# A third staging tile for the weight slices, scratch rows of the maxima moved into another tile, and a larger constant per transfer in the planner

## The chip, the cores and the metric

The kernel runs on one core of a Trainium2 chip. The metric is the device time of one execution in microseconds. The engines that matter are TensorE (PE, matmuls), VectorE (DVE), ScalarE (ACT), and SyncE (SP), whose queue issues every transfer of this kernel in program order.

## What is computed

An attention layer with a decay bias feeds two feed-forward layers with 2304 tokens, model width 512 and hidden width 2048. Cut to what matters:

```python
scores = scale * np.matmul(q, k.transpose(0, 1, 3, 2))          # 4 x 8 heads, 576 x 576, head width 64
bias = -(cum[:, :, :, None] - cum[:, :, None, :])               # cum: running sum of max(s, 0)
scores = np.where(causal, -1000000000.0, scores + np.minimum(bias, 0.0))
scores = scores - np.max(scores, axis=-1, keepdims=True)
attn = np.exp(scores)
attn = attn / (np.sum(attn, axis=-1, keepdims=True) + 1e-09)
x = np.matmul(attn, v)                                          # heads side by side: 2304 x 512
h = x @ w_in;  x = (h * np.cos(h)) @ w_out                      # first feed-forward layer
h = x @ w_in2; x = (np.maximum(h, 0.0) + np.log1p(np.exp(-np.abs(h)))) @ w_out2
```

## The kernel before, in words

The program is a list of operations (`P.op`), each with a due time `vt`, the tiles that it reads and writes, and one or two engines that may do it. `Planner.plan` turns this list into one instruction order for each engine: it steps through time with a cost for every operation and gives a free engine the ready operation with the earliest due time. On the chip only these orders remain: each engine works through its own in sequence and waits on semaphores where an input is late. For a transfer, the planner adds the time to issue it, 640 ns, its bytes at 360 per ns, and a constant (line 183, 770 ns) before it counts as landed.

Attention runs as 32 units (batch by head). For each unit PE makes the scores twice: once coarsely for the row maxima (line 510 on DVE: a masked maximum, with a scratch output in the tile `junk` that nobody reads; line 516 collects them), and once exactly for the exponential (line 564 on ACT). The product with v is copied out by line 538 (ACT, into `num`) and sent to the DRAM tile `adram`. After every fourth unit the sums of the rows come back as the tile `rd`, get 1e-9 added and are inverted (lines 591 and 592, DVE), and go out again. `emit_x` (lines 620, 298, 307) loads the normalised x for the feed-forward layers and splits it into a high and a low part, `xh` and `xl`.

A feed-forward layer works on token blocks of 512 (one of 256) and on 16 chunks `f` of the hidden width. For each chunk: 12 matmuls (w_in with xh and xl) into one of the banks that the program calls bank_65 to bank_68; an activation over several steps on ACT and DVE (layer one: lines 657, 658, 660, 662, 664; layer two: lines 669 to 676); its result is split into `ghi` (line 298, ACT) and `glo` (line 307, DVE); then 12 matmuls with w_out into bank_69 to bank_72. In the first layer the matmuls of a later chunk need the bank that line 664 has read.

The weights come in 64-bit slots of 1024 words of 32 bit (`wide`), 64 slices of 512 KB: 2 layers, 16 chunks, w_in and w_out. `emit_weights` turns each slice into a high and a low part: transfer into `stage`, then line 422 (ACT, absolute value, into `conv`), lines 424, 426, 429 and 432 (DVE), the high part (line 298, ACT) and the low part (line 307 or 308, DVE), into `wearly` or `wlate`. Slices take `stage` 0 and 1 in turn, so the transfer of a slice waits until line 432 has read the slice before the previous one. `conv` has two tiles too. The first layer's slices are worked through during attention and up to some 300 us; the second layer's replace the first's from 528 us on, chunk by chunk as the first layer's last block has used them.

Of the kernel before, what the change touches and what calls it, by code (L numbers as in the profile page):

```python
# [10 lines left out]
BF16 = mybir.dt.bfloat16  # L11
U32 = mybir.dt.uint32
# [10 lines left out]
QS = (0, 256, 576)  # L23
EARLY, SLOT = 8, 4992
GUARD = True
TUNE = dict(lam=61.3799, mu=21.9699, sub1=-0.8, sp4=-0.47, ld4=-2.57, load=-3.32, vload=0.3081, split=-0.462, max=-0.4135, s=1.63, av=2.34,
            norm=3.5, md=0.14, sd=0.22, ud=5900.0, e=1.2214, o=2.5648, end=3.5, x0=30.0, xd=2364.0, wa=5.755, wb=4.1769,
            wc=1479.6, wd=9828.5, wg=9000.0, pre=9606.0, we=16928.0, wf=6383.3, backlog=1292.7, hz=16175.7)
# [15 lines left out]
class Planner:  # L44
# [49 lines left out]
    def plan(self, penalty=4000.0):  # L94
# [7 lines left out]
        dma_free = 0.0  # L102
# [14 lines left out]
        while left:  # L117
            progress = False
            wake = []
            for e in free:  # L120
                if free[e] > t:
                    continue
                q = pend[e]
                while q and q[0][0] <= t:
                    _, sq, i, o = heapq.heappop(q)
                    if o.eng is None:
                        avail[e].append((o.vt, sq, i, o))
                a = [x for x in avail[e] if x[3].eng is None]
                avail[e] = a
                if not a:  # L130
                    if e == PE and self.filler and t >= self.filler_from:
                        o = Op()
                        o.seq, o.vt, o.eng, o.start, o.reads, o.writes, o.deps, o.succ = -1, t, PE, t, (), (("warm", 0),), set(), []
                        cold = t < self.filler_from + 5000.0
                        o.fn = self.filler
                        o.end = free[PE] = t + (215.0 if cold else 110.0)
                        tail = 107.0
                        order.append(o)
                        progress = True
                    continue  # L140
                if e in (DVE, ACT) and not force:
                    a = [x for x in a if x[0] <= reach + TUNE["hz"]]
                    if not a:
                        continue
                if e == PE and any(k == ("bank", 7) for k, _ in a[0][3].writes):
                    self.filler = None
                if e == SP and dma_free - t > TUNE["backlog"] + 0.01:
                    a = [x for x in a if x[3].opts[0][2].transfer < 300.0]
                    if not a:
                        wake.append(dma_free - TUNE["backlog"])  # L150
                        continue
                if e == ACT:
                    best = min(a, key=lambda x: (x[0] + (penalty if x[3].table and x[3].table != table else 0.0), x[1]))
                elif e == PE:
                    left_over = max(0.0, tail - (t - free[PE]))
                    fast = [x for x in a if x[3].opts[0][2].load < 100.0]

                    def score(x):
                        f = x[3].opts[0][2]
                        then = 54.0 if len(fast) > (f.load < 100.0) else LDW  # L160
                        return x[0] + TUNE["lam"] * max(0.0, f.load - left_over) + TUNE["mu"] * max(0.0, then - f.tail)

                    best = min(a, key=lambda x: (score(x), x[1]))
                else:
                    best = min(a, key=lambda x: (x[0], x[1]))
                _, _, i, o = best
                _, d, fn = o.opts[i]
                cost = d
                if e == PE:
                    reach = max(reach, o.vt)  # L170
                    cost += max(0.0, fn.load - left_over)
                    tail = fn.tail
                if e == ACT and o.table and o.table != table:
                    cost += self.SWITCH
                    table = o.table
                    switches += 1
                o.eng, o.fn, o.start = e, fn, t + (cost - d if e == PE else 0.0)
                free[e] = t + cost
                busy[e] += cost
                o.end = t + cost  # L180
                if e == SP:
                    dma_free = max(dma_free, t + d + 640.0) + fn.transfer
                    o.end = dma_free + 770.0
                order.append(o)
                left -= 1
                progress = True
                for s in o.succ:
                    s.ready = max(s.ready, o.end + min(self.hop(e, x[0]) for x in s.opts))
                    s.ndep -= 1
                    if s.ndep == 0:  # L190
                        push(s)
            if progress:
                force = False
            else:
                nxt = [f for f in free.values() if f > t]
                nxt += [pend[e][0][0] for e in free if pend[e] and pend[e][0][0] > t and free[e] <= t]
                nxt += wake
                force = not nxt
                if force:
                    continue  # L200
                assert nxt, [(o.vt, o.reads, o.writes) for o in ops if o.eng is None][:5]
                t = min(nxt)
# [22 lines left out]
def build(tc, qk, v, s, w1, w2, out):  # L225
# [8 lines left out]
    def T(name, shape, dt=F32):  # L234
        return sb.tile(shape, dt, name=name, tag=name)
# [8 lines left out]
    wide = w1.dtype != F32  # L244
# [5 lines left out]
    raws = [T(f"raw{i}", [128, 2, S]) for i in range(2)]  # L250
    xst = [raws[0][:, i, 0:512] for i in range(2)]
    rst = [raws[1][:, i, 0:512] for i in range(2)]
    stage = [T(f"stage{i}", [128, 1024], U32) for i in range(2)] if wide else []
    conv = [T(f"conv{i}", [128, 512], U32 if wide else F32) for i in range(2)]
    ghi = [T(f"ghi{i}", [128, 512], F32R) for i in range(2)]
    glo = [T(f"glo{i}", [128, 512], F32R) for i in range(2)]
# [4 lines left out]
    bc = T("bc", [128, 2, S])  # L261
# [6 lines left out]
    ident = T("ident", [128, 128], BF16)  # L268
    tri = T("tri", [128, 128], BF16)
    zero = T("zero", [128, 256], BF16)  # L270
    junk = [T(f"junk{i}", [128, (384, 512)[i]], BF16) for i in range(2)]
    mxp = T("mx", [128, 2, 10])
    mx = [mxp[:, i] for i in range(2)]
    mr = [xl[1][:, i, 0:128] for i in range(3)]
# [67 lines left out]
    for i in range(3):  # L342
        o = i * SLOT
# [31 lines left out]
    def warm():  # L375
# [14 lines left out]
         r=[(nk[0], "spos")], w=[(nk[1], "cum")])  # L390
# [6 lines left out]
    stage_n = [0]  # L397
# [9 lines left out]
    def emit_weights(which, f, at):  # L407
        w = (w1, w2)[which]
        tag = (which, f)
        for half, (hi, lo, scale, nm) in enumerate(((wih[f], wil[f], 2.0 if which else None, "wi"), (woh[f], wol[f], None, "wo"))):  # L410
            i = stage_n[0] % 2
            stage_n[0] += 1
            cv = conv[i]
            vs_ = at(f + half * 0.5)
            wsrc = w[f, :, half * 512:half * 512 + 512]
            if wide:
                sg = stage[i]
                dma(at(f + half * 0.5 - 0.7), sg, wsrc.bitcast(U32), r=[("go", 0)], w=[(("st", i), (tag, half))])
                pr = sg.rearrange("p (n t) -> p n t", t=2)
                cf = cv.bitcast(F32)  # L420
                if GUARD:
                    P.op(vs_ - 2, [(ACT, act_t(512), lambda cf=cf, pr=pr: A.activation(cf, pr[:, :, 1].bitcast(F32), AF.Abs))],  # L422
                         r=[(("st", i), (tag, half))], w=[(("cv", i), (tag, half, -2))])
                    P.op(vs_ - 1, [(DVE, dve_t(512, fast=True), lambda cf=cf: V.tensor_scalar(cf, cf, HI_MIN, HI_MAX, op0=ALU.max, op1=ALU.min))],
                         r=[(("cv", i), (tag, half, -2))], w=[(("cv", i), (tag, half, -1))])
                P.op(vs_, [(DVE, dve_t(512, fast=True), lambda cv=cv, hs=cv if GUARD else pr[:, :, 1]: V.tensor_scalar(  # L426
                    cv, hs, 3, 0x3FFFFFFF, op0=ALU.logical_shift_left, op1=ALU.bitwise_and))],
                    r=[(("st", i), (tag, half))] + ([(("cv", i), (tag, half, -1))] if GUARD else []), w=[(("cv", i), (tag, half, 0))])
                P.op(vs_ + 1, [(DVE, dve_t(512), lambda cv=cv, pr=pr: V.scalar_tensor_tensor(  # L429
                    cv, pr[:, :, 1], 0xC0000000, cv, op0=ALU.bitwise_and, op1=ALU.bitwise_or))],  # L430
                    r=[(("st", i), (tag, half)), (("cv", i), (tag, half, 0))], w=[(("cv", i), (tag, half, 1))])
                P.op(vs_ + 2, [(DVE, dve_t(512), lambda cv=cv, pr=pr: V.scalar_tensor_tensor(  # L432
                    cv, pr[:, :, 0], 29, cv, op0=ALU.logical_shift_right, op1=ALU.bitwise_or))],
                    r=[(("st", i), (tag, half)), (("cv", i), (tag, half, 1))], w=[(("cv", i), (tag, half))])
                src = cv.bitcast(F32)
            else:
                dma(at(f + half * 0.5 - 0.7), cv, wsrc, r=[("go", 0)], w=[(("cv", i), (tag, half))])
                src = cv
            sk = slot_keys(f) if which == 0 else []
            P.op(vs_ + 3, copy_opts(hi, src, 512, scale=scale, engines=(ACT,)),  # L440
                 r=[(("cv", i), (tag, half))], w=[((nm, "h", f), tag)] + sk)
# [353 lines left out]
```

## Time and profile before

| | |
|---|---|
| Runs | 1022.13, 1023.58, 1024.79 us; median 1023.58 |
| Profiled execution | 1024.17 us, of which 1022.4 us are the span from the first to the last instruction |
| PE | busy 1006.6 us (98% of the span) |
| DVE, ACT | busy 701.5 and 613.8 us (69% and 60%) |
| HBM | 66.87 MB read, 18.64 MB written |
| Mean granted clock of TensorE | 0.995 of 2.4 GHz |

An engine's busy time is the union of its instructions. A number in brackets behind an instruction is the time that its engine idled before it, with what ended the wait. PE's share hides that the span consists of stages with different limits, so the stages are what to read.

### The profile page before, as it was taken

What the parts mean: (1) busy time and instruction counts of PE and PEld (TensorE: products, weight loads), DVE (VectorE), ACT (ScalarE), POOL (GpSimd) and SP (SyncE); (2) the same over time, 40 slices, a digit from 0 to 9 for tenths busy, and PEclk for the clock granted to TensorE, in tenths of its full rate; (3) what the DMA queues carried; (4) which work ended last, traced back from release to release, by engine and by line L of the source; (5) the groups of instructions that cost most, each with busy time, mean ns of one, the idle gap of its engine ahead of it and who ended that gap; (6) DMA issues with size and microseconds to landing.
All of it is one profiled execution on the core that took longest, in us unless ns stands there. A gap on an engine that the chain in (4) does not pass through costs nothing.

```text
span 1022.4 us, 14520 instructions
## 1 busy us (share of the span) xinstructions
PE 1006.6 (98%) x5179; PEld 844.5 (83%) x5179; DVE 701.5 (69%) x1441; ACT 613.8 (60%) x1129; POOL 49.4 (5%) x67
## 2 busy tenths in 40 slices
PE   8999999999999999999999998999999999999998
PEld 7888788877888889988888886888888998888886
DVE  8799898969974545545458999975564756545553
ACT  4777777767765545555456668664455555554444
POOL 8112111100000000000000000000000000000000
PEclk9999999999999999999999999999999999999999
DMA  5766666773522222102014435310230200001001
GB/s 164 223 184 201 169 181 189 190 198 114 170 83 83 62 83 82 44 21 62 1 43 136 152 124 175 124 62 1 83 105 9 84 1 23 19 1 42 1 1 41
DMA packets 45098, 95.31 MB, mean 93 GB/s; under 512 B 7586, under 2 KB 14242, under 8 KB 45026
## 3 DMA queue, kind: packets, MB, share of 16 engines
q1 hardware_dynamic: 45026, 94.39, 30.4%
q8 instruction: 40, 0.66, 0.3%
q14 instruction: 32, 0.26, 0.1%
HBM read 66.87 MB, written 18.64 MB: 84 GB/s over the span
## 4 chain that ended last, share of the span: by engine, by line
PE 81%; DMA 8%; DVE 5%; ACT 3%; issue 2%; POOL 1%; SPq 0%; ACTq 0%; DVEq 0%; POOLq 0%
PE bank L321 80%; DMA stage<-w 5%; DMA adram<-num 2%; PE bank L376 1%; DMA rd<-adram 1%; DVE conv L429 1%; ACT conv L422 1%; DVE junk L510 1%; DMA raw<-adram 1%; DVE pf L664 0%; DVE conv L432 0%; DVE conv L426 0%; POOL wlate L329 0%; DVE glo L307 0%; ACT pf L564 0%
## 5 line engine op out<-in xcount | busy, mean ns | idle before, releaser
L321 PE MATMUL bank<-xh,wearly 128*128 128x512 f32 (+1 forms) x640 | 195.5, 371 | 3.8 <-DVE pf L664 3.8
L321 PE MATMUL bank<-ghi,wearly 128*128 128x512 f32 (+1 forms) x640 | 194.9, 370 | 1.3 <-ACT ghi L298 1.3
L321 PE MATMUL bank<-ghi,wlate 128*128 128x512 f32 (+1 forms) x640 | 193.4, 368 | 0.6 <-ACT ghi L298 0.6
L321 PE MATMUL bank<-xh,wlate 128*128 128x512 f32 (+1 forms) x640 | 193.6, 368 | 0.0
L298 ACT ACTIVATE ghi<-pf 128x512 fp32r<-128x512 f32 (+1 forms) x160 | 94.1, 588 | 145.8 <-DVE pf L676 97.5
L307 DVE TENSOR_TENSOR glo<-pf,ghi 128x512 fp32r<-128x512 f32 (+1 forms) x160 | 101.9, 637 | 78.2 <-ACT ghi L298 77.6
L321 PE MATMUL bank<-wlate 128*128 128x320 f32 (+9 forms) x576 | 149.4, 362 | 2.9 <-POOL xl L329 1.7
L321 PEld LDWEIGHTS bank<-xh,wearly 128*128 128x128 f32 x640 | 118.1, 190 | 24.9 <-DVE pf L664 4.5
L321 PEld LDWEIGHTS bank<-ghi,wearly 128*128 128x128 f32 x640 | 118.0, 190 | 21.8 <-ACT ghi L298 1.7
L321 PEld LDWEIGHTS bank<-ghi,wlate 128*128 128x128 f32 x640 | 117.2, 189 | 20.9 <-ACT ghi L298 1.0
L321 PEld LDWEIGHTS bank<-xh,wlate 128*128 128x128 f32 x640 | 117.2, 189 | 19.9
L321 PE MATMUL bank<-pf,vf 128*65 128x320 f32 (+4 forms) x448 | 126.4, 384 | 0.8 <-ACT pf L564 0.8
L321 PE MATMUL bank<-glo,wlate 128*128 128x512 f32 (+1 forms) x320 | 118.1, 369 | 1.2 <-DVE glo L307 1.2
L321 PE MATMUL bank<-glo,wearly 128*128 128x512 f32 (+1 forms) x320 | 118.5, 370 | 0.2 <-DVE glo L307 0.2
L321 PE MATMUL bank<-xl,wearly 128*128 128x512 f32 (+1 forms) x320 | 118.4, 370 | 0.0
L321 PE MATMUL bank<-xl,wlate 128*128 128x512 f32 (+1 forms) x320 | 117.7, 368 | 0.0
L672 DVE SCALAR_TENSOR_TENSOR bc<-pf 128x512 f32<-128x512 f32 (+1 forms) x80 | 51.0, 638 | 86.1 <-ACT pf L670 86.0
L321 PEld LDWEIGHTS bank<-wlate 128*128 128x128 f32 (+1 forms) x576 | 94.6, 192 | 17.9 <-DVE mx L510 2.8
L660 DVE SCALAR_TENSOR_TENSOR pf<-pf,pf 128x512 f32<-128x512 f32 (+1 forms) x80 | 50.8, 635 | 54.8 <-ACT pf L658 54.7
L510 DVE CUSTOM_DVE_ANT_0 junk<-bank,mask 128x384 bf16<-128x384 f32 (+3 forms) x192 | 81.8, 468 | 9.3 <-PE bank L321 7.8
L564 ACT ACTIVATE pf<-bank 128x256 f32<-128x256 f32 (+2 forms) x160 | 67.0, 431 | 33.1 <-PE bank L321 24.7
L669 ACT ACTIVATE pf<-bank 128x512 f32<-128x512 f32 (+1 forms) x80 | 44.3, 554 | 67.7 <-PE bank L321 65.1
(79 smaller groups left out, 1370.2 us busy)
## 6 DMA issues: line engine op xcount, KB each, us to landing
stage<-w SPq DMA_DIRECT2D x64, 512.0 KB
raw<-qk SPq DMA_DIRECT2D x15, 576.0 KB
wlate<-wlate SPq DMA_DIRECT2D x30, 288.0 KB
vf<-v SPq DMA_DIRECT2D x32, 160.0 KB
adram<-num SPq DMA_DIRECT2D x32, 146.2 KB
xdram<-num SPq DMA_DIRECT2D x18, 256.0 KB
out<-num SPq DMA_DIRECT2D x18, 256.0 KB
raw<-adram SPq DMA_DIRECT2D x32, 128.0 KB
```

Source lines behind the costliest of these rows:

```text
L298: opts.append((ACT, act_t(n, psum), (lambda: A.activation(o, i, AF.Copy, scale=1.0 if scale is None else scale))))
L307: return [(DVE, dve_t(n), lambda: V.tensor_tensor(o, a, hi.bitcast(F32), op=ALU.subtract))]
L321: X.matmul(o, a, b, start=st, stop=sp, skip_group_check=skip)
L376: X.matmul(bank[7][:, 0:256], zero[:, 0:128], zero, start=True, stop=True)
L422: P.op(vs_ - 2, [(ACT, act_t(512), lambda cf=cf, pr=pr: A.activation(cf, pr[:, :, 1].bitcast(F32), AF.Abs))], r=[(("st", i), (tag, half))] ...
L429: P.op(vs_ + 1, [(DVE, dve_t(512), lambda cv=cv, pr=pr: V.scalar_tensor_tensor(cv, pr[:, :, 1], 0xC0000000, cv, op0=ALU.bitwise_and, op1=A ...
L510: P.op(tx + 1, [(DVE, dve_t(w, True) + DX, lambda bk=bk, off=off, w=w, mo=mo, col=col, pr=pr, jk=junk[i if x < 2 else x - 2]: V.tensor_ten ...
L564: P.op(tx + 3, [(ACT, act_t(wt, True) + AX, lambda pt=pt, bk=bk, wt=wt: A.activation(pt[:, :wt], bank[bk][:, :wt], AF.Exp))], r=[(("bank", ...
L660: P.op(te + 2, [(DVE, dve_t(n), lambda a0=a0, a1=a1: V.scalar_tensor_tensor(a1, a1, MAGIC, a0, op0=ALU.subtract, op1=ALU.subtract))], r=[( ...
L669: P.op(te, [(ACT, act_t(n, True), lambda a0=a0, hp=hp: A.activation(a0, hp, AF.Abs, scale=0.5))], r=hr, w=[(k0, (tg, "a"))])
L672: P.op(te + 2, [(DVE, dve_t(n), lambda a0=a0, a2=a2: V.scalar_tensor_tensor(a2, a0, 2.0, a0, op0=ALU.subtract, op1=ALU.mult, reverse0=True))],
```

## The change

A third tile `stage` is made, and slices take the three in turn; `conv` keeps its two. The scratch rows of the masked maxima, which had two tiles `junk` of their own, are now the first halves of the two rows of `bc`, a tile that is otherwise used in the second feed-forward layer only (line 672). A slice's transfer gets a due time 1.2 instead of 0.7 chunk steps ahead of its conversion. The planner counts 1250 ns instead of 770 ns for the last part of every transfer, of all kinds, which shifts the orders on all engines.

```diff
+STG = 1.2
...
                 if e == SP:
                     dma_free = max(dma_free, t + d + 640.0) + fn.transfer
-                    o.end = dma_free + 770.0
+                    o.end = dma_free + 1250.0
...
-    stage = [T(f"stage{i}", [128, 1024], U32) for i in range(2)] if wide else []
+    stage = [T(f"stage{i}", [128, 1024], U32) for i in range(3)] if wide else []
...
-    junk = [T(f"junk{i}", [128, (384, 512)[i]], BF16) for i in range(2)]
+    junk = [bc[:, i, 0:256].bitcast(BF16) for i in range(2)]
...
             if wide:
-                sg = stage[i]
-                dma(at(f + half * 0.5 - 0.7), sg, wsrc.bitcast(U32), r=[("go", 0)], w=[(("st", i), (tag, half))])
+                j = (stage_n[0] - 1) % 3
+                sg = stage[j]
+                dma(at(f + half * 0.5 - STG), sg, wsrc.bitcast(U32), r=[("go", 0)], w=[(("st", j), (tag, half))])
...
-                         r=[(("st", i), (tag, half))], w=[(("cv", i), (tag, half, -2))])
+                         r=[(("st", j), (tag, half))], w=[(("cv", i), (tag, half, -2))])
```

The last pair stands for five: lines 422, 426, 429 and 432 read `("st", j)` likewise. New lines shift the numbers: line 591 of before is 593 of the changed kernel, 432 is 434, 664 is 666, and so on. In the rows below `stage_87` to `stage_88` (before) and `stage_87` to `stage_89` (changed) are the staging tiles; `conv_89`, `pf_95`, `ghi_91`, `num_101` of before are `conv_90`, `pf_96`, `ghi_92`, `num_102` of the changed kernel. All engines keep the same set of instructions, except that two of the copies of finished banks move from ACT to DVE; PE's 5,240 are the same ones.

First place: DVE at the end of attention, from the row sums of the last four units to the product of the first layer's first chunk (line 664, then 666), which frees bank_65. Before:

```order
L591 TENSOR_SCALAR rd<-rd 128x18
L307 TENSOR_TENSOR xl_84<-raw_85,xh_82 128x512
L592 RECIPROCAL rd<-rd 128x18
L432 SCALAR_TENSOR_TENSOR conv_90<-stage_88,conv_90 128x512
L664 TENSOR_TENSOR pf_95<-bank_65,pf_97 128x512
```

After:

```order
L593 TENSOR_SCALAR rd<-rd 128x18
L308 TENSOR_TENSOR wlate<-conv_90,wlate 128x512
L594 RECIPROCAL rd<-rd 128x18
L431 SCALAR_TENSOR_TENSOR conv_91<-stage_89,conv_91 128x512
L662 SCALAR_TENSOR_TENSOR pf_98<-pf_98,pf_96 128x512
L434 SCALAR_TENSOR_TENSOR conv_91<-stage_89,conv_91 128x512
L622 TENSOR_TENSOR raw_85<-raw_85,raw_86 128x512
L426 TENSOR_SCALAR conv_90<-conv_90 128x512
L662 SCALAR_TENSOR_TENSOR pf_99<-pf_99,pf_97 128x512
L666 TENSOR_TENSOR pf_96<-bank_65,pf_98 128x512
```

Between the row sums and the product stood three instructions, and now stand eight.

Second place: ACT at the start of the second layer, from the conversion of a slice (line 422, then 424) to the high part of that layer's first chunk (`ghi_91`, then `ghi_92`), whose matmuls PE needs next. Before:

```order
L671 ACTIVATE pf_97<-pf_95,lnb 128x512
L298 ACTIVATE xh_81<-raw_85 128x512
L669 ACTIVATE pf_96<-bank_66 128x512
L422 ACTIVATE conv_89<-stage_87 128x512
L298 ACTIVATE num_101<-bank_69 128x512
L298 ACTIVATE wlate<-conv_90 128x512
L298 ACTIVATE num_101<-bank_70 128x512
L298 ACTIVATE ghi_91<-pf_95 128x512
```

After:

```order
L673 ACTIVATE pf_98<-pf_96,lnb 128x512
L424 ACTIVATE conv_91<-stage_88 128x512
L671 ACTIVATE pf_97<-bank_66 128x512
L299 ACTIVATE num_102<-bank_69 128x512
L299 ACTIVATE ghi_92<-pf_96 128x512
```

Two copies stood between the slice and the high part besides the first copy out of bank_69, and these two now come later.

Third place: DVE in attention, around the fifth batch of row sums. Before:

```order
L510 ISA junk_110,mx<-bank_67,mask 64x256
L510 ISA mx 64x1
L591 TENSOR_SCALAR rd<-rd 128x18
L510 ISA junk_109,mx<-bank_69,mask 128x384
L510 ISA mx 128x1
L592 RECIPROCAL rd<-rd 128x18
L510 ISA junk_110,mx<-bank_65,mask 128x512
L510 ISA mx 128x1
```

After:

```order
L512 ISA bc,mx<-bank_67,mask 64x256
L512 ISA mx 64x1
L512 ISA bc,mx<-bank_69,mask 128x384
L512 ISA mx 128x1
L512 ISA bc,mx<-bank_65,mask 128x512
L512 ISA mx 128x1
L593 TENSOR_SCALAR rd<-rd 128x18
```

The row sums, which wait for a transfer, moved behind the last two maxima of the unit.

## Rows read from the trace of the kernel before

**Rows 1.** The page, part 1: busy time, share of the span, instructions of each engine.

```profile
PE 1006.6 (98%) x5179; PEld 844.5 (83%) x5179; DVE 701.5 (69%) x1441; ACT 613.8 (60%) x1129; POOL 49.4 (5%) x67
```

**Rows 2.** Busy time by stretch: us, PE, PEld, DVE, ACT, POOL, clock, DMA, GB/s.

```profile
0.00:25.00 25.00, 22.11 (x155) 17.75 (x156) 20.95 (x58) 11.95 (x15) 20.59 (x37) 0.93 0.55 160
...
110.00:190.00 80.00, 78.75 (x488) 64.23 (x487) 70.46 (x216) 58.38 (x128) 11.87 (x13) 1.00 0.68 187
...
210.00:240.00 30.00, 25.45 (x114) 20.17 (x113) 22.12 (x42) 19.01 (x37) 0.00 (x0) 0.94 0.58 168
...
610.00:640.00 30.00, 26.82 (x108) 20.93 (x107) 28.50 (x53) 24.23 (x43) 0.00 (x0) 0.94 0.51 172
...
1015.00:1022.40 7.40, 3.67 (x17) 2.70 (x15) 0.51 (x1) 2.39 (x4) 0.00 (x0) 1.00 0.37 142
```

**Rows 3.** PE alone by stretch: us, PE busy (instructions), granted clock, DMA share, GB/s.

```profile
226.00:236.00 10.00, 6.21 (x21) 0.83 0.53 154
610.00:620.00 10.00, 8.33 (x36) 1.00 0.55 180
626.00:636.00 10.00, 8.50 (x30) 0.83 0.64 224
```

**Rows 4.** Timeline of PE: start, us, instruction, idle time before it and releaser.

```profile
213.41 0.49 PE L321 MATMUL bank<-pf,vf 128*65 128x256 f32 x1 [0.77 <-ACT pf L564]
...
232.17 0.80 PE L321 MATMUL bank<-xh,wearly 128*128 128x512 f32 x1 [3.79 <-DVE pf L664]
...
617.85 0.50 PE L321 MATMUL bank<-glo,wlate 128*128 128x512 f32 x1 [1.08 <-DVE glo L307]
...
630.08 0.51 PE L321 MATMUL bank<-ghi,wearly 128*128 128x512 f32 x1 [1.28 <-ACT ghi L298]
```

**Rows 5.** The chain that ended last, pieces at 220 to 231 and 605 to 630 us.

```profile
220.94 4.59 DMA adram<-num
...
225.59 4.41 DMA rd<-adram
...
609.15 3.22 DMA stage<-w
...
621.99 5.28 DMA stage<-w
```

**Rows 6.** Waits of the whole run: waiter, waited for, us in total, times, longest.

```profile
ACT conv L422 <- DMA stage<-w: 26.2, 25, 2.5
...
DVE rd L591 <- DMA rd<-adram: 6.1, 6, 1.8
...
PE bank L321 <- DVE mx L510: 1.1, 3, 0.5
```

**Rows 7.** The issuing queue's own waits, whole run.

```profile
SPq L283 <- DVE conv L432: 203.6, 49, 51.6
```

**Rows 8.** Waits of DVE from 530 to 632 us.

```profile
DVE conv L424 <- ACT conv L422: 3.4, 6, 1.0
...
DVE wlate L307 <- ACT wlate L298: 1.3, 2, 1.0
```

**Rows 9.** Timeline of ACT at 219 to 221 and 627 to 630 us.

```profile
219.42 0.66 ACT L422 ACTIVATE conv<-stage 128x512 f32<-128x512 f32 x1 [2.55 <-DMA stage<-w]
...
627.35 0.68 ACT L422 ACTIVATE conv<-stage 128x512 f32<-128x512 f32 x1 [1.67 <-DMA stage<-w]
...
629.41 0.62 ACT L298 ACTIVATE ghi<-pf 128x512 fp32r<-128x512 f32 x1
```

**Rows 10.** Timeline of DVE at 230 to 232 and 611 to 613 us.

```profile
230.03 0.18 DVE L591 TENSOR_SCALAR rd<-rd 128x18 f32<-128x18 f32 x1 [1.78 <-DMA rd<-adram]
...
231.43 0.68 DVE L664 TENSOR_TENSOR pf<-bank,pf 128x512 f32<-128x512 f32 x1
...
611.63 0.69 DVE L660 SCALAR_TENSOR_TENSOR pf<-pf,pf 128x512 f32<-128x512 f32 x1
612.23 0.69 DVE L432 SCALAR_TENSOR_TENSOR conv<-stage,conv 128x512 uint32<-128x512 uint32 x1
```

More of the change, by code (lines that the diff above doesn't have):

```diff
@@ L427, in emit_weights @@
                     cv, hs, 3, 0x3FFFFFFF, op0=ALU.logical_shift_left, op1=ALU.bitwise_and))],
-                    r=[(("st", i), (tag, half))] + ([(("cv", i), (tag, half, -1))] if GUARD else []), w=[(("cv", i), (tag, half, 0))])
+                    r=[(("st", j), (tag, half))] + ([(("cv", i), (tag, half, -1))] if GUARD else []), w=[(("cv", i), (tag, half, 0))])
                 P.op(vs_ + 1, [(DVE, dve_t(512), lambda cv=cv, pr=pr: V.scalar_tensor_tensor(
                     cv, pr[:, :, 1], 0xC0000000, cv, op0=ALU.bitwise_and, op1=ALU.bitwise_or))],
-                    r=[(("st", i), (tag, half)), (("cv", i), (tag, half, 0))], w=[(("cv", i), (tag, half, 1))])
+                    r=[(("st", j), (tag, half)), (("cv", i), (tag, half, 0))], w=[(("cv", i), (tag, half, 1))])
                 P.op(vs_ + 2, [(DVE, dve_t(512), lambda cv=cv, pr=pr: V.scalar_tensor_tensor(
                     cv, pr[:, :, 0], 29, cv, op0=ALU.logical_shift_right, op1=ALU.bitwise_or))],
-                    r=[(("st", i), (tag, half)), (("cv", i), (tag, half, 1))], w=[(("cv", i), (tag, half))])
+                    r=[(("st", j), (tag, half)), (("cv", i), (tag, half, 1))], w=[(("cv", i), (tag, half))])
                 src = cv.bitcast(F32)
```

## Prediction

> **What bounds the kernel now.** I read the busy shares first, then the busy time by stretch, then the waits inside the stretches where PE idles. PE is busy 1006.6 of 1022.4 us [rows 1], so all that the span can lose while PE does the same matmuls is 15.8 us of idle time, plus what PE loses at a lower clock. By stretch [rows 2] the idle time is 2.9 us in the first 25, 1.25 from 110 to 190, 4.55 from 210 to 240, 3.18 from 610 to 640 and 3.73 in the last 7.4. The first and the last part are start and final copies, which the change leaves alone. The other 850 us hold only 0.2 of it. Two stretches also have a low granted clock: 0.83 over 226 to 236 and over 626 to 636 [rows 3], which at the lower level of 1.2 GHz is 3.4 us at half rate, or 1.7 us lost each time. In both, PE had just stood still, 3.79 us before 232.17 and 1.28 us before 630.08 [rows 4]; in 610 to 620, with 1.67 us idle, the clock stayed at 1.00 [rows 3]. What can be won is thus 1.25 + 4.55 + 3.18 + 3.4, or 12.4 us.
>
> What ends these gaps? In attention three of PE's waits are for the maxima, 1.1 us in all, and DVE itself stands 6.1 us in line 591 for the row sums `rd` [rows 6]: the maxima queue behind it. At 213 PE waits 0.77 us for an exponential, at 232 it waits for line 664 to free bank_65 [rows 4]. Ahead of line 664 the chain of the end runs through two transfers, `adram` 4.59 us and `rd` 4.41 us [rows 5], whose start, the last copy on ACT, stood behind a conversion that waited 2.55 us for its slice [rows 9]. Line 591 then sat 1.78 us until `rd` was there, and line 664 follows 1.40 us after it [rows 10]. At 617.85 PE waits for `glo`, on a DVE that is busy 28.50 of 30 us [rows 2, 4]. At 630.08 it waits for `ghi`, which ACT began at 629.41, after a conversion that had idled 1.67 us for its slice [rows 4, 9].
>
> **The change part by part.** The third tile: the issuing queue stands 203.6 us in 49 waits for line 432 to free a staging tile [rows 7], and ACT stands 26.2 us in 25 waits for a slice, 2.5 us at most [rows 6]. With three tiles a transfer waits for the slice three back, not two. Between 610 and 630 a slice gives DVE five instructions, with products between them; at a step of 0.60 us (two starts in [rows 10]) one slice more is 3 us of lead, above the longest wait. I therefore take ACT's slice waits as gone. Free of them, DVE gets back 3.4 us in line 424 and 1.3 us in line 307 between 530 and 632 [rows 8], 4.7 us in all.
>
> Against that, conversions run further ahead in DVE's order. Counted in the orders over the last 13 chunks of the first layer, from `glo` to `glo`, before has 131 instructions, the changed kernel 134: three more, at 0.60 us each 1.8 us. Net, DVE is 2.9 us ahead when the products at 617 to 630 are due. PE's idle time there is 3.18 us, so 0.3 us remain, and a gap that short need not cost clock, as the 1.67 us in 610 to 620 did not. The second place in the order helps: `ghi` passes two copies. Gain 2.9 + 1.7 = **4.6 us**. Bounds: all of it, 4.9; or, if no wait goes and the three instructions only add, 1.8 lost.
>
> The longer count: `rd` moves behind two maxima in four of the eight batches, the third place in the order, so DVE does the maxima in the time that it now waits, and PE's 1.1 us for them go. Gain **1.0 us**; bounds 1.25 (all of that stretch) and 0, since PE may also wait elsewhere for a unit's changed order.
>
> The end of attention: without the slice wait the 0.77 us at 213 go. The last copy can come 2.55 us earlier, and `rd` is read at 230.03 - 2.55 = 227.5. But between it and the product that frees bank_65 the order now has eight instructions in place of three, five more, 3.0 us. So the product starts at 227.5 + 1.4 + 3.0 = 231.9, not 231.43: 0.5 later, with the low clock behind it as now. Attention's own gains, 1.0 and 0.77, start the chain earlier and carry through. Net **0.3 us** gained here. Bounds: 3.0 lost, if `rd` lands no earlier than now; 4.55 + 1.7 = 6.2 gained, if nothing is waited for.
>
> Transfers themselves: once issued, a slice takes 3.22 to 5.28 us [rows 5]. The planner's count for the same, from the code (0.64, 1.46 for 512 KB, and the constant), was 2.9 and is 3.35, so the old one was always short and the new one suits only the quick ones; the third tile's lead has to cover the rest. By the Trainium skill, "DMA: Bandwidth & Descriptors", section on the anatomy of one DMA, a transfer takes about 2.0 us plus its bytes at 436 GB/s (given for another issuing path), an estimate of 3.2 us here: the old count would have left 25 waits of 0.3 us, 7.5 in place of 26.2, and the gain of 4.6 would shrink to some 1.3. The trace agrees with that for its shortest transfer alone.
>
> The scratch rows cost nothing: `bc` is used by DVE alone and holds data in the second layer only, long after the last maximum, and the maxima's shapes stay. The two copies that go from ACT to DVE are two 128x512 instructions, at 0.69 us each [rows 10] 1.4 us on an engine that is busy 69% of the span [rows 1]; uncovered they would cost those 1.4 us. What is late next: with staging no longer short, `conv` with its two tiles is, and the conversion on ACT then waits for lines 307 and 308.
>
> Sum: 4.6 + 1.0 + 0.3 = 5.9 us off the profiled 1024.17 gives 1018.3; the median of the runs shown is 0.6 below that execution, so **1017.7 us**.
>
> **The rivals.** *Hidden anyway (no change).* DVE is 95% busy where PE waits [rows 2], and its work is not smaller. If DVE's gaps only turn from slice waits into waits for ACT or for `conv`, the first layer's end keeps its gaps; only 630.08, directly behind a slice wait, gains, 1.28 + 1.7, and the end of attention loses some of it. For it: DVE's 3.4 and 1.3 us are a small part of ACT's 26.2, most of which was harmless. Against it: [rows 9] show the wait in front of `ghi` itself. Time: 1023.6 - 3.0 to 1023.6 + 2, about 1023. Part of this is that the change does not do what it says, if the single issuing queue holds slices back for other transfers; 203.6 us of its waits at line 432 speak against that.
>
> *Conversions crowd out products (slower).* One mechanism, in DVE's order: slices ready earlier are taken ahead of the products for which PE waits. Five instructions at 231 us cost 3.0, three at 617 us cost 1.8: 1023.6 + 4.8 = 1028.4. It decides if `rd` is read after 229.5 and DVE between 530 and 632 wins back less than 1.8 us.
>
> *Both stretches cured (much faster).* If `rd` is read before 225.5 (faster transfers with fewer beside them), line 666 is no longer late: up to 12.4 off, with 3 to 6 more than forecast likelier, 1012 to 1015.
>
> **How the numbers follow.** Forecast 0.50 (its own range 1015.5 to 1020.5), no change 0.27, crowding 0.11, both cured 0.12. About 0.3%, 3.1 us, is what a measurement of this kernel can tell. Nearly all of forecast and all of "both cured" lie below 1020.5: 0.61 faster; most of "no change" and the forecast's upper edge 0.28 the same; crowding 0.11 slower. The range runs from 1013.5, inside "both cured", to 1024.5, inside "no change", leaving out about 0.05 and 0.15.
>
> **What would show it.** ACT's waits for slices: 26.2 us falls below 8. The queue's wait for the staging read (line 434 now) falls. DVE from 530 to 632 wins over 2 us, PE from 610 to 640 is busy 29 us or more with the clock at 1.00. PE's waits for maxima fall to 0.5 or less. PE still stands 3 us or more around 230, for line 666, with a clock of 0.83 after it. I am wrong if slices are still waited for, if a new wait for `conv` stands in front of `ghi`, or if PE stands longer than 5 us near 230.

## The result and the profile after

The changed kernel takes 1012.25 us (median of 4 runs, 1009.28 to 1012.83); the kernel before, run beside it on the same chip, takes 1022.86 us (1019.36 to 1024.79). The ratio is 0.9894, 95% interval 0.9861 to 0.9928: 10.6 us faster by the medians. Forecast were 5.9 us, to 1017.7, and a range that began at 1013.5. The direction was right, the gain is nearly twice as large, and the time lies just below the range. The profiled execution took 1012.16 us, with a span of 1010.5 and a mean granted clock of 0.998.

The busy time by stretch, columns as in [rows 2]; the last two lines are those of PE alone, as in [rows 3]:

```profile
0.00:25.00 25.00, 21.97 (x165) 17.89 (x165) 22.17 (x60) 12.85 (x17) 21.73 (x37) 1.00 0.65 192
...
110.00:190.00 80.00, 79.53 (x497) 65.75 (x495) 70.18 (x219) 58.95 (x130) 14.84 (x14) 1.00 0.71 187
...
210.00:240.00 30.00, 26.81 (x117) 21.75 (x116) 28.46 (x55) 23.02 (x41) 0.00 (x0) 0.94 0.60 177
580.00:610.00 30.00, 30.00 (x134) 24.86 (x133) 30.00 (x58) 23.67 (x40) 0.00 (x0) 1.00 0.44 147
610.00:640.00 30.00, 30.00 (x134) 24.86 (x133) 29.96 (x56) 24.13 (x43) 0.00 (x0) 1.00 0.49 161
...
10.00:15.00 5.00, 5.00 (x43) 1.00 0.67 195
...
226.00:236.00 10.00, 8.95 (x33) 0.83 0.45 136
```

Two stretches of the kernel before that the prediction did not read, PE alone, same columns:

```profile
10.00:15.00 5.00, 5.00 (x30) 0.66 0.66 188
...
580.00:610.00 30.00, 29.84 (x131) 1.00 0.38 123
```

Read the instruction counts beside the busy times. Between 580 and 640 PE runs 268 matmuls of one shape where it ran 239. At 30.00 / 134 = 0.224 us each, the 29 more are 6.5 us. By idle time and clock the same stretch of before had lost 3.18 + 0.16 + 1.7 = 5.0. Busy time counts as work what lies between modelled matmul ends, which is the likely rest. At the start the clock is 1.00 over 10 to 15 us where it was 0.66, worth 0.34 x 5 = 1.7 us. Attention from 110 to 190 has 0.8 us more of PE, and 210 to 240 has 1.4. That places 6.5 + 1.7 + 0.8 + 1.4 = 10.4 of the 11.9 us between the two spans.

Comparing the start of the n-th matmul places all of it. Both traces hold 5,179 matmuls, so the n-th of each says how far the work has come. By this measure the start gives 1.9 us, attention up to 210 us 1.7, the end of attention 1.7 and the start of the second layer 6.7. Attention up to 210 gave more than the 1.25 us that PE had idled in it [rows 2].

The waits after, columns as in [rows 6]; the last line is DVE's from 530 to 632 us, as in [rows 8]:

```profile
PE bank L322 <- DVE pf L666: 3.2, 1, 3.2
...
DVE rd L593 <- DMA rd<-adram: 1.4, 2, 1.0
...
ACT conv L424 <- DVE wlate L308: 5.0, 8, 1.3
...
SPq L284 <- DVE conv L434: 187.4, 49, 51.6
...
DVE conv L426 <- ACT conv L424: 0.7, 1, 0.7
```

The slice waits of ACT, 26.2 us in [rows 6], have no line left among ACT's sixty longest, nor has PE's wait for the maxima among PE's. Waits of ACT for `conv` have come in. One of 1.30 us stands at 625, ahead of the `ghi` at 627.68, and it costs nothing, since PE is full from 580 to 640. One gap stays at the end of attention. The chain there, after: start, us, what.

```profile
214.47 4.59 DMA adram<-num
219.12 3.02 DMA rd<-adram
...
222.94 0.17 DVE rd L594
...
225.80 0.60 DVE pf L662
226.39 0.61 DVE pf L666
227.01 0.04 issue
227.05 7.96 PE bank L322 x27
```

`rd` lands at 222.14, and the product stands at 226.39, 4.2 us behind it, where 1.4 us lay between them before [rows 5, 10]. PE waits 3.2 us for it and then works at a clock of 0.83. All of it is some 5 us earlier than before: `adram` begins 6.5 us earlier (220.94 in [rows 5]), `rd` travels 3.02 us instead of 4.41, and 2.8 us of this are lost again to the longer row of DVE.

### The profile page after: what moved, and what is told of

The parts are those of the page before. It is cut to its first block, busy times and chain, and to the rows that moved or that the text cites. A ratio compares the mean times of both kernels' runs of the same rounds, so it can differ in the third digit from the quotient of the medians.

```text
span 1010.5 us, 14525 instructions
## 1 busy us (share of the span) xinstructions
PE 999.6 (99%) x5179; PEld 842.9 (83%) x5179; DVE 698.8 (69%) x1443; ACT 615.0 (61%) x1127; POOL 51.7 (5%) x67
## 4 chain that ended last, share of the span: by engine, by line
PE 93%; DMA 3%; DVE 2%; POOL 1%; ACT 1%; issue 1%; SPq 0%; DVEq 0%; POOLq 0%; ACTq 0%
PE bank L322 93%; DMA wlate<-wlate 1%; DMA raw<-adram 1%; POOL wlate L330 1%; DVE bc L512 0%; DMA adram<-num 0%; PE bank L377 0%; DMA rd<-adram 0%; SPq L284 0%; ACT pf L566 0%; POOL tri L365 0%; DVE wlate L494 0%; DVE wearly L308 0%; DVE raw L622 0%; ACT wlate L485 0%
## 5 line engine op out<-in xcount | busy, mean ns | idle before, releaser
L299 ACT ACTIVATE ghi<-pf 128x512 fp32r<-128x512 f32 (+1 forms) x160 | 94.1, 588 | 145.8 <-DVE pf L678 97.0
L512 DVE CUSTOM_DVE_ANT_0 bc<-bank,mask 128x256 bf16<-128x256 f32 (+2 forms) x192 | 81.7, 469 | 8.7 <-PE bank L322 6.0
```

The costliest lines, as they stand in the source:

```text
L299: opts.append((ACT, act_t(n, psum), (lambda: A.activation(o, i, AF.Copy, scale=1.0 if scale is None else scale))))
L512: P.op(tx + 1, [(DVE, dve_t(w, True) + DX, lambda bk=bk, off=off, w=w, mo=mo, col=col, pr=pr, jk=junk[i if x < 2 else x - 2]: V.tensor_ten ...
```

## Experiments

Twelve kernels in three groups of four. Within a group all ran on one chip beside the kernel before, with medians of 1022.49, 1021.76 and 1021.78 us for it. None leaves out any of the computation. All medians in one table (us; the ratio is to the kernel before in the same group):

| label | staging tiles | constant, ns | median (lowest to highest) | ratio, 95% interval |
|---|---|---|---|---|
| tile_same_order | 3, orders of two | 770 | 1017.21 (1013.90 to 1017.95) | 0.9941 (0.9921 to 0.9961) |
| tile_alone | 3 | 770 | 1017.33 (1014.76 to 1018.52) | 0.9939 (0.9919 to 0.9960) |
| count_alone | 2 | 1250 | 1009.74 (1008.03 to 1013.26) | 0.9876 (0.9853 to 0.9899) |
| tile_count | 3 | 1250 | 1013.22 (1010.40 to 1014.22) | 0.9904 (0.9885 to 0.9924) |
| after_rd_late | 3 | 1250 | 1011.11 (1008.53 to 1013.35) | 0.9889 (0.9867 to 0.9911) |
| count_slices | 2 | 1250 for slices | 1016.19 (1015.19 to 1019.18) | 0.9947 (0.9928 to 0.9966) |
| count_rest | 2 | 1250 for the others | 1015.53 (1014.61 to 1017.24) | 0.9936 (0.9920 to 0.9953) |
| count_2000 | 2 | 2000 | 1006.83 (1006.63 to 1007.05) | 0.9849 (0.9830 to 0.9869) |
| tile_second_layer | 3 in layer two | 1250 | 1010.56 (1009.35 to 1011.82) | 0.9895 (0.9881 to 0.9909) |
| tile_2000 | 3 | 2000 | 1007.76 (1007.21 to 1009.19) | 0.9872 (0.9854 to 0.9890) |
| count_start | 2 | 1250 in the first 15 us | 1020.67 (1019.41 to 1022.25) | 0.9991 (0.9982 to 1.0000) |
| count_2500 | 2 | 2500 | 1010.99 (1010.02 to 1011.15) | 0.9897 (0.9882 to 0.9912) |

How far each profile is ahead of that of the kernel before, in us, stage by stage. The stages end where PE's 159th, 1,302nd, 1,547th and 3,419th matmul starts (before at 25.45, 210.05, 270.09 and 660.21 us); every trace in the table holds 5,179:

| profile of | start | attention to 210 us | end of attention | start of layer two |
|---|---|---|---|---|
| changed kernel | 1.9 | 1.7 | 1.7 | 6.7 |
| tile_same_order | 1.2 | 1.2 | 1.5 | 6.4 |
| tile_alone | -1.6 | -0.6 | 1.1 | 6.7 |
| count_alone | 2.0 | 2.7 | 5.0 | 6.6 |
| tile_count | 1.9 | 2.6 | 0.4 | 6.7 |
| count_slices | 0.0 | -0.3 | 0.2 | 5.7 |
| count_rest | 1.6 | 2.7 | 2.0 | 2.5 |
| tile_second_layer | 1.3 | 2.5 | 2.0 | 6.7 |
| count_start | 1.1 | -0.5 | -0.3 | 3.2 |

The end of attention stands for all up to 270.09 us. Each row is one execution. How much such rows can vary shows in count_start: behind the start its orders are those of before, and it is still 3.2 us ahead at the second layer. The profiled execution of the kernel before took 1024.17 us, above its median, so the differences to it are on the large side.

**The third tile with the orders of before.** The planner goes on planning two tiles, the transfers use three, and the scratch rows lie in `bc`.

```diff
-    stage = [T(f"stage{i}", [128, 1024], U32) for i in range(2)] if wide else []
+    stage = [T(f"stage{i}", [128, 1024], U32) for i in range(3)] if wide else []
-    junk = [T(f"junk{i}", [128, (384, 512)[i]], BF16) for i in range(2)]
+    junk = [bc[:, i, 0:256].bitcast(BF16) for i in range(2)]
-                sg = stage[i]
+                sg = stage[(stage_n[0] - 1) % 3]
```

> Before's orders on all engines and before's planner, but the slices rotate through three staging tiles (scratch rows in bc). Lead theory (what was missing was room for the next slice): ACT's waits for slices fall from 26.2 to under 8 us, PE from 610 to 640 is nearly full, and the end of attention gains 0 to 2 us: 5 to 8 us off, 1015 to 1018. Order theory (the planner's new orders do it, from the larger count): in-order queues still hold the readers where they were, under 2 us off, 1021 to 1023.

1017.21, 5.3 us less. PE alone by stretch, columns as above:

```profile
226.00:236.00 10.00, 6.32 (x27) 1.00 0.56 162
610.00:640.00 30.00, 30.00 (x133) 1.00 0.52 173
```

Its waits:

```profile
ACT conv L422 <- DMA stage<-w: 9.0, 9, 2.2
```

With not one instruction moved, 610 to 640 is full. 9.0 us of slice waits remain, a little more than the 8 expected, and they harm nothing there. So the tile's own depth is worth its 5.3 us by itself; the scratch rows, which move too, were not tried alone.

**The third tile planned, constant 770.** The change without the larger constant and with the old due time of 0.7 chunk steps.

```diff
-STG = 1.2
+STG = 0.7
-                    o.end = dma_free + 1250.0
+                    o.end = dma_free + 770.0
```

> The third tile is planned for, with the old count of 770 ns and the old due step of 0.7. Lead theory: as the third tile in kept orders or better, 1014 to 1017. Order theory: PE keeps its waits for maxima and for the products, 1019 to 1023.

1017.33, just above the range of the first theory. Its waits:

```profile
ACT conv L424 <- DMA stage<-w: 1.2, 1, 1.2
...
DVE rd L593 <- DMA rd<-adram: 4.4, 4, 2.3
...
PE bank L322 <- DVE mx L512: 1.3, 3, 0.5
```

Slice waits all but gone, and no gain over the kernel that kept 9.0 us of them. The waits for `rd` (6.1 us before) and for the maxima (1.1) stay, as the second theory had it.

**The constant alone, two tiles.**

```diff
-                    o.end = dma_free + 770.0
+                    o.end = dma_free + 1250.0
```

> Two tiles and the old due step, but 1250 ns in the planner's count. Lead theory: slices are still waited for (over 15 us on ACT), only the waits for row sums in attention go, about 1 us: 1021 to 1022.5. Order theory: readers stand later in the queues, so nothing stands in front of ghi: 5 to 8 us off, 1015 to 1018.

1009.74, 12.8 us less, with the old two staging tiles: far below what either theory gave. Busy time by stretch:

```profile
210.00:240.00 30.00, 28.99 (x127) 23.18 (x127) 27.20 (x52) 22.14 (x39) 0.00 (x0) 1.00 0.58 169
...
610.00:640.00 30.00, 30.00 (x134) 24.84 (x133) 29.95 (x56) 23.69 (x42) 0.00 (x0) 1.00 0.49 166
```

The chain at the end of attention:

```profile
218.28 3.32 DMA rd<-adram
...
221.62 0.19 DVE rd L591
...
221.83 0.27 DVE rd L592
222.09 0.22 DVE pf L664
```

The product stands directly behind the two operations on `rd`, and in this profile PE no longer waits for it at all. 610 to 640 is full here too, while ACT still stands 8.4 us in 12 waits for slices. Either part of the change alone cures that stretch, and the second one to come adds nothing to it.

**Tile and constant, old due time.** The changed kernel with 0.7 in place of 1.2.

```diff
-STG = 1.2
+STG = 0.7
```

> The changed kernel with the old due step of 0.7 for slices. If the due step is idle, since with three tiles a slice is fetched as soon as a tile is free, within 1 us of the changed kernel, 1011 to 1013.5. If slices were fetched earlier by it, ACT waits for slices again and PE idles from 610 to 640: 1015 to 1018.

1013.22, against 1012.25 of the whole change in another group; the two ratios overlap nearly whole. The traces fit that: PE, DVE, ACT and POOL work through the same orders in both, and only two transfers in the first 23 us are placed otherwise. The due time does next to nothing, and this is nearly a second measurement of the changed kernel.

Against the tile with 770 on the same chip the constant brings 4.1 us. Between the two profiles 3.5 us lie in the start, where the tile with 770 had drawn a clock of 0.50, 3.2 in attention up to 210 us, and nothing is gained behind it. PE's idle time does not show all that attention lost. The waits of its weight loads (PEld) show more; line 512 is the masked maximum, line 518 collects the maxima. With 770:

```profile
PEld bank L322 <- DVE mx L512: 3.1, 6, 0.9
...
PEld bank L322 <- DVE xl L518: 1.5, 4, 0.6
```

And with 1250:

```profile
PEld bank L322 <- DVE xl L518: 0.5, 2, 0.3
...
PEld bank L322 <- DVE mx L512: 0.5, 2, 0.3
```

DVE's own wait for `rd` falls from 4.4 to 1.5 us, so the queue behind `rd` in attention is the likely cause; no run moves `rd` alone. At the transition PE stands 3.8 us for line 666 and the clock of 210 to 240 is 0.89. The median is 3.5 us above that of the constant alone, with runs that overlap.

**`rd` behind the product.** The changed kernel, with the last unit's two operations on `rd` and the store of `rd` due later.

```diff
+        late = 20000.0 if u == NB * NH - 1 else 0.0
...
-        P.op(tn + 2, [(DVE, 160.0, lambda: V.tensor_scalar_add(rdt, rdt, 1e-9))], ...
+        P.op(tn + 2 + late, [(DVE, 160.0, lambda: V.tensor_scalar_add(rdt, rdt, 1e-9))], ...
```

> The changed kernel with one edit: the last unit's two rd operations (the first addition and the reciprocal) and the store of rd to DRAM get a due time 20000 later, so VectorE's row has the first product of the transition ahead of them instead of behind. Theory that the third tile's small gain at the end of attention is lost because rd waits for its 9 KB transfer in front of the product: TensorE's wait of 3.2 us for the product goes to under 1.0, the granted clock in 210 to 240 us goes from 0.94 to 0.99 or more, and 1012.25 becomes 1007.5 to 1009.5. Rival, that the third tile's earlier conversions in VectorE's row hold up the product and rd does not: TensorE still waits 2 us or more for the product, and the time is 1011 to 1013.5.

1011.11, within the rival's range. PE still waits for the product:

```profile
PE bank L322 <- DVE pf L667: 2.3, 1, 2.3
```

The chain of this kernel:

```profile
222.20 0.47 DVE pf L663
...
222.72 0.23 DVE conv L434
...
223.32 0.69 DVE raw L623
224.01 0.34 DVE conv L426
224.34 0.60 DVE pf L663
224.94 0.61 DVE pf L667
```

With `rd` out of the way, operations of the slices' conversion and a normalisation stand between the phase steps (line 663) and the product (line 667). That is the mechanism which the prediction called crowding. Taking `rd` away brings 1.1 us of median, within the spread, and 2.3 of the 3.2 us of PE's wait stay: in this profile most of the wait is not `rd`'s. What the crowding costs the whole kernel is not measured by this run.

**The constant for the slices alone, and for the rest alone.** Two tiles; `count` replaces the constant, 1250 for one set and 770 for the other.

```diff
-                    o.end = dma_free + 770.0
+                    o.end = dma_free + fn.count
...
+        go.count = 1250.0 if w and w[0][0][0] == "st" else 770.0
```

> The kernel before with two staging tiles, and 1250 instead of 770 as the constant of the weight slices alone; all other transfers keep 770. Theory that the stretch of the second layer's conversions is cured by slices that are counted later, and the end of attention by rd that is counted later: the stretch gives its 6.1 to 6.6 us, TensorE 610 to 640 has 29.8 us or more, rd still stands ahead of the product and the end of attention gives 0 to 2, so 1022.5 becomes 1014.5 to 1016.5. Rival, that the gain comes from the other transfers (inputs, rd and its way through DRAM): 1021 to 1024 and TensorE 610 to 640 at 26 to 27 us.

> The kernel before with two staging tiles, 770 kept for the weight slices, and 1250 for all other transfers. Theory of two places: the second layer's conversions keep their lost 6.1 to 6.6 us (TensorE 610 to 640 at 26 to 27 us of 30), and the end of attention gives 2 to 6.6, depending on how many rows stand between rd and the product (four here, none with 1250 for all): 1016 to 1020.5. Rival, that one set of transfers carries all of the gain: 1009 to 1012 if it is this set. Second rival, that the nine more filler matmuls at the start, which this kernel has and the one with 1250 for slices alone has not, are worth 2 us: 1020.5 with nothing else moved.

1016.19 and 1015.53: 5.6 and 6.2 us less. The first is in the range expected, the second 0.5 us below it; that one set carries all of the gain is out. The parts of 0.53% and 0.64% add up to 1.17%, against 1.24% for all transfers together. Busy time by stretch with 1250 for the slices:

```profile
210.00:240.00 30.00, 25.47 (x115) 20.34 (x114) 24.00 (x46) 19.86 (x38) 0.00 (x0) 0.94 0.65 185
...
610.00:640.00 30.00, 29.76 (x131) 24.15 (x130) 29.95 (x56) 25.59 (x45) 0.00 (x0) 1.00 0.55 180
```

And with 1250 for the rest:

```profile
0.00:25.00 25.00, 21.92 (x165) 17.86 (x165) 21.84 (x60) 12.51 (x17) 20.59 (x37) 1.00 0.61 172
...
210.00:240.00 30.00, 27.23 (x117) 21.90 (x116) 26.14 (x50) 20.88 (x37) 0.00 (x0) 0.94 0.58 173
...
610.00:640.00 30.00, 28.01 (x116) 22.41 (x115) 29.02 (x54) 22.38 (x39) 0.00 (x0) 0.94 0.48 158
```

The slices cure the start of the second layer and leave the rest of the kernel as it was (5.7 us in the stage table, and within 0.3 elsewhere). The others gain in the start (1.6), in attention (2.7) and at its end 2.0, the least that was expected there: PE still waits 2.8 us for the product. Their 2.5 at the second layer is no more than count_start shows with the orders of before. How a later count cures 610 to 640 is seen on ACT's timeline with 1250 for the slices (columns as in [rows 9]):

```profile
623.36 1.10 ACT L299 ACTIVATE num<-bank 128x512 f32<-128x512 f32 x2
624.32 0.66 ACT L299 ACTIVATE ghi<-pf 128x512 fp32r<-128x512 f32 x1
624.84 0.69 ACT L423 ACTIVATE conv<-stage 128x512 f32<-128x512 f32 x1
```

`ghi` goes ahead of the conversion. In [rows 9] the conversion, which had to wait 1.67 us for its slice, stood ahead of three copies and of `ghi`. The larger number thus changes what waits behind a slice. Whether it also changes when slices come was not measured.

**The constant at the start alone.** 1250 for transfers that the planner starts in its first 15 us. The planner fills the longer idle time there with 43 instead of 34 matmuls on zeros before the first product. ACT's order is that of before.

```diff
-                    o.end = dma_free + 770.0
+                    o.end = dma_free + (1250.0 if t < 15000.0 else 770.0)
```

> The kernel before with the constant of 1250 for transfers that the planner starts in its first 15 us, and 770 for all later ones. TensorE then has nine more filler matmuls ahead of its first product, and the order behind the start is that of before: ScalarE's row is the same, VectorE's and the queue's differ in a line or two. Theory that the longer idle time counted at the start, filled with more matmuls, keeps the clock up there and is worth the 1.9 us that the traces show: 1022.3 becomes 1020 to 1020.8, all else as before. Rival, that the clock of the first 15 us differs from one execution to the next whatever the kernel (it was 1.00 and 0.50 with the old start): 1021.7 to 1023, and the missing 2 us lie in attention.

1020.67, 1.1 us less by the medians and 0.9 by the ratio, with an interval that reaches from 1.8 us to nothing. The clock of the first 25 us was 1.00 in its profile. The median is in the range of the first theory; of the 1.9 us about half came.

**Larger constants, two tiles.** 2000 and 2500.

```diff
-                    o.end = dma_free + 770.0
+                    o.end = dma_free + 2000.0
```

> The kernel before with two staging tiles and a constant of 2000 instead of 770 for every transfer. In VectorE's row the first product of the transition now stands four rows ahead of the first rd operation, so rd's wait can hold nothing at the transition. Theory that the queue order at two places is what counts: TensorE's waits at the transition stay under 1 us, 610 to 640 stays at 30.0 us of TensorE, and the time is that of 1250 alone or less, 1007 to 1010.5. Rival, that 1250 fits by chance and each constant shuffles the order anew: a new wait of over 3 us somewhere and 1012 to 1020.

> The kernel before with two staging tiles and a constant of 2500 for every transfer. VectorE's row has the product three rows ahead of the first rd operation. Theory that from the point on where nothing in a row waits for a transfer the count is flat: 1006 to 1008.5, waits of TensorE at the transition under 1 us. Rival, that a count above the real landing times (the weight slices took 3.2 to 5.5 us from issue to landing, the planner now counts about 4.6 us) leaves engines idle or orders useful work late: 1009 or more.

1006.83 with 2000, better than the changed kernel by 5 us and than 1250 alone by 3, with four runs within 0.42 us. 1010.99 with 2500, the rival's figure. Waits with 2000:

```profile
PE bank L321 <- DVE pf L664: 0.7, 1, 0.7
...
ACT conv L422 <- DMA stage<-w: 2.9, 4, 1.3
```

And with 2500:

```profile
PE bank L321 <- POOL wlate L524: 2.1, 1, 2.1
PE bank L321 <- DVE pf L664: 1.8, 1, 1.8
...
ACT conv L422 <- DMA stage<-w: 2.8, 3, 2.2
```

The slice waits no longer fall, and two new waits come in, 2.1 us for POOL in the first 25 us and 1.8 us at the end of attention. The theory that the time is flat from some point on is wrong. That a count too long orders other work behind is the likely reason; which rows do that was not followed up.

**Third tile in the second layer alone.** With 1250; the first layer's slices take two tiles, so that DVE's order at the end of attention is that of the constant alone.

```diff
-                j = (stage_n[0] - 1) % 3
+                j = (stage_n[0] - 1) % (3 if which else 2)
...
-                dma(at(f + half * 0.5 - STG), ...
+                dma(at(f + half * 0.5 - (STG if which else 0.7)), ...
```

> The changed kernel with the third staging tile used in the second layer alone; the first layer, which overlaps the end of attention, turns two tiles with the old due time. VectorE's row at the transition is then that of the kernel with the count alone: the last rd, its reciprocal and the product stand directly behind one another. Theory that the third tile costs at the transition, by conversions that it lets into VectorE's row ahead of the product: TensorE's wait there goes from 3.2 us to under 1.0, the clock of 210 to 240 us to 1.00, and 1012.25 becomes 1009 to 1010.5. Rival, that the third tile costs elsewhere (more transfers at once in the second layer, scratch rows in another tile): 1011.5 to 1013.5.

1010.56, between the two theories. PE waits 1.6 us for line 666, with the clock at 0.94 in 210 to 240, where the constant alone had no such wait and a clock of 1.00. Up to 523 us the orders of PE, DVE, ACT and POOL are the same in both kernels; one transfer near 22 us and the place of the scratch rows differ. So the orders of the engines do not explain the 3 us between them at the end of attention (2.0 and 5.0 in the stage table), and this does not settle whether the third tile costs there.

**The third tile with 2000.** The changed kernel with 2000.

```diff
-                    o.end = dma_free + 1250.0
+                    o.end = dma_free + 2000.0
```

> The changed kernel with a constant of 2000 in place of 1250. VectorE's row has the product ahead of rd, but conversion operations that the third tile lets in still stand among the three phase operations ahead of it. Theory that these conversions hold the product up, rd or no rd: TensorE still waits 1.5 to 3 us for the product and the time is 1008.5 to 1011, above that of 2000 with two tiles (1006.83). Rival, that a count long enough makes the third tile harmless: 1006 to 1007.5 and a wait under 1 us.

1007.76, closer to the rival. Busy time by stretch:

```profile
210.00:240.00 30.00, 30.00 (x135) 24.01 (x134) 28.12 (x54) 24.73 (x43) 0.00 (x0) 1.00 0.66 193
```

The conversions stand in DVE's order ahead of the product as before, and PE does not wait for it: with 2000 the same crowding holds the product up no longer. Against 1006.83 with two tiles the third one brings nothing that shows.

## Why the prediction was wrong, by its own steps

**The third tile, 4.6 us.** Right in mechanism and a little small: 5.3 us by the medians, and by the ratio 4.0 to 8.1. The upper bound of 4.9 lies under the median, because it summed idle time and clock. Counted in matmuls the stretch had more to give, 6.5 us in the profiles; but that execution of before may have lost more there than others do, since count_start, with the same orders in that stretch, lost 3.2 us less. Not foreseen was that the constant, by moving `ghi` ahead of the conversions, cures the same stretch with two tiles, so that 4.6 is no term of the tile's alone. By the Trainium skill, "DMA: Bandwidth & Descriptors", section on the anatomy of one DMA, the prediction had put a slice at an estimated 3.2 us and the gain at 1.3. The runs disagree: the third tile with the orders of before still had 9.0 us of slice waits, more than the 7.5 of that estimate, and gained 5.3 by depth alone, so the sum of these waits is no measure of the gain.

**The longer count, 1.0 us.** This is the failed step: its mechanism is borne out as far as the waits show it (PE's waits for the maxima are gone), its price is not. With the third tile in place the constant is worth 4.1 us (1017.33 to 1013.22), where this term and the end of attention had 1.3. The step took as all that attention could give the 1.25 us that PE idles from 110 to 190. In the stage table attention up to 210 us is shorter by 1.7 us in the changed kernel and by 2.5 to 2.7 in the four other runs in which all transfers, or all but the slices, have 1250; with 770 it is -0.6 to 1.2. count_rest has this gain, count_slices and count_start have not, so it belongs neither to the slices nor to the start. Part of the queue behind `rd` stood in the weight loads' waits, which the prediction did not read. How much of the gain is that queue, and how much the earlier or later place of other work, is not separated.

**The start, priced at nothing.** The sentence "start and final copies, which the change leaves alone" does not hold. The prediction's own [rows 2] have a clock of 0.93 in the first 25 us, which its list of low clocks leaves out; with nine more filler matmuls they had their full clock, and count_start puts this at 1.1 us. So the ceiling of 12.4 us for all that can be won was too low too: the constant alone took 12.8, and 2000 ns took 14.9.

**The end of attention, 0.3 us.** "`rd` is read at 230.03 - 2.55 = 227.5", less the 1.0 and 0.77 of attention's gains, is 225.7. It lands at 222.14: the chain begins 6.5 us earlier where these three make 4.3, and `rd` travels 1.4 us less. "Five more instructions, 3.0 us" measured 2.8, the prediction's most exact number. The gap in front of the product was foreseen with its size (3 us or more; 3.2) and the clock behind it (0.83). The end of attention gained 1.7 us in the changed kernel's profile and 0.4 in that of its near twin tile_count, so the 0.3 is not far off; what lies ahead of it was underrated.

**The rivals.** *Both stretches cured* gave 1012 to 1015 and had "`rd` read before 225.5" as its condition. Condition and time came true, at a chance of 0.12; its mechanism did not, since line 666 is still late. *Crowding* is real at the product (2.3 us of wait without `rd`), but the kernel is faster all the same. *Hidden anyway* is out.

**The signs.** Every one of the forecast came true: no slice waits, DVE busy 100.6 of 102 us from 530 to 632 where it was 94.1, PE full from 610 to 640, no wait for maxima, 3.2 us at 227 with a clock of 0.83. One sign of being wrong came up as well, a wait for `conv` ahead of a `ghi`, and cost nothing. All of them speak of where the sum looked; none could show what it had left out.

**Open.** Whether the third tile takes back something with 1250: medians of 1013.22 and 1012.25 stand against 1009.74, with overlapping runs. The first two are nearly one kernel, and the wait at the transition comes and goes with the same orders on the engines.

## What to carry to other kernels

A constant that a planner adds to every transfer moves work at every place where a queue runs in order: split it by kind of transfer and by stage, the start included, before it gets a small price. Price a stretch by the instructions that it is short of, or by when the n-th starts, not by the idle time shown. And before memory is spent on a deeper buffer, try the planner's assumed landing time: with two tiles, 2000 ns were worth 15 us, while the third tile with 770 was worth 5 and with 2000 nothing.

## What the runs showed of the hardware

The clock of the start differs between executions with the same filler. With 34 filler matmuls it was 0.66 from 10 to 15 us in the kernel before, and 0.50 in the planned third tile:

```profile
10.00:15.00 5.00, 5.00 (x24) 0.50 0.68 194
```

In the third tile with the orders of before, also with 34, it was 1.00. With 43 it was 1.00 in each of the seven profiles of such kernels.

The length of a stall does not tell the clock behind it. With the orders of before and three tiles PE stood 3.1 us for the product and 226 to 236 us had a clock of 1.00; with the third tile in the second layer alone it stood 1.6 us for it and 1.1 us for `glo` soon after, and the same stretch had 0.83.

The spread of a kernel's runs often goes with the mean granted clock, but not always. Of the changed kernel's four runs, the one at 1.000 took 1009.28 us, and the three at 0.998 took 1012.16 to 1012.83. Of the constant of 2000 all four ran at 1.000 and lie within 0.42 us, while the kernel before, at 0.992 to 0.998 beside them, spread over 5.6 us. But with the constant at the start alone the one run at 1.000 was the longest of eleven, 1022.25 us.
